# Attention and FFN in one kernel: a shorter lead-in, values sent in 128 rows, and another written order of the opening

## The chip, the cores and the metric

The kernel runs on one core of a Trainium2 chip. The core has a matrix engine (TensorE, PE in the profile; its weight loads are listed apart as PEld), a vector engine (VectorE, DVE), an activation engine (ScalarE, ACT), a general engine (GpSimd, POOL) and a queue processor that issues the DMA transfers here (SyncE, SP). Each engine works through its own list of instructions in order and waits on semaphores for the others. The metric is the device time of one execution in microseconds (us).

## The reference

The kernel computes attention for 8 batches, 8 heads, 576 positions and 64 channels per head, and then a two-layer FFN with GELU on the result. Heads 0 to 3 are local (each position sees the last 32), heads 4 to 7 are strided (each position sees every 32nd before it).

```python
scores = scale * np.matmul(q, k.transpose(0, 1, 3, 2))
mask_local = (rel >= 0) & (rel < stride)
mask_strided = (rel >= 0) & (pos[None, :] % stride == pos[:, None] % stride)
scores = np.where(masks[None, :, :, :], scores, -1000000000.0)
...
attn = np.exp(scores)
attn = attn / (np.sum(attn, axis=-1, keepdims=True) + 1e-09)
attn_out = np.matmul(attn, v).astype(np.float32)
...
x = np.ascontiguousarray(attn_out.transpose(0, 2, 1, 3)).reshape(B * S, H * D)
h = x @ w_in
g = 0.5 * h * (1.0 + erf(h * inv_sqrt2))
return (g @ w_out).astype(np.float32)
```

x has 4608 rows of 512 channels; w_in is 512 x 2048 and w_out 2048 x 512, all in float32.

## The kernel before

The 4608 rows are cut into 9 tiles of 512. For a tile the FFN goes through 16 slices of 128 hidden channels. For each slice `ffn_h` multiplies into the bank H (lines 655 to 657: 4 channel blocks times 3 products, since each float32 operand is split into a high and a low part so that the fast matmul keeps the precision), `ffn_g` applies GELU, and `ffn_o` multiplies into four banks O (lines 694 to 696, 12 matmuls). This is the bulk of TensorE's work. The 16 slices of the weights come by one DMA each (`load_w`, ws, 1 MB) and are split on chip by ScalarE and VectorE (`split_w`, lines 155 to 170, five steps: lead, word, other, high part, low part).

The attention of a tile must be done before its FFN. For every tile but the first, local heads are computed by `band_job` and strided heads on VectorE (`strided_qk`, line 526, and `strided_av`, line 571). The first tile has its own path, since TensorE has nothing else to do then. Its local heads run in four jobs (`local_job`): scores (L289) from qk, softmax on VectorE and ScalarE (L247 to L268), transposes (L295), copies (L297) and the product with the values (L303, `jv`, from vl). Its strided heads run on TensorE too: scores (L416) in two halves from qka, softmax (L425 to L439), transposes (L443), copies (L445), the product with the values va (L459, 64 small matmuls in the program), a transpose on VectorE (L464), and the split into the high part dh (L467, ScalarE) and the low part dl (L470, VectorE). After that the first H can start.

The values of the local heads are laid out by the host as `vl`: for each block of queries 96 keys (`LK`, 64 of the block and 32 before it) by 512 numbers, 192 KB. Blocks 0 to 3, those of the first tile, are loaded one by one (`load_jv`); later tiles load four at once (`load_values`, line 229).

Up to slice 16 the order of work on four of the engines is written by hand, in the table `START`. Each word is one step: w0 is the load of weight slice 0, q0 and v0 loads of local job 0, S and B the loads of the strided heads' q, k and v of the first tile, K1 and V1 those of the next tile's keys and values, E the strided heads' first q and k, L0 the next step of local job 0, a0 and b0 steps of the two halves, A0 of the strided product, c0 a step of the split of weight slice 0, f0 a step of the FFN with slice 0, s, x and y steps of the next tile's local heads, u and r steps of the strided ones. Each step issues its instructions on the engines that it needs, so the table sets the order within each engine's list, SP's queue of DMAs among them. GpSimd's order is not in it. Ahead of the table stand some matmuls on zeros, the lead-in (line 780), and the making of masks.

Eight semaphores tell of the landing of SP's DMAs in turn, so a DMA also waits for the one eight before it when that has not landed.

Of the kernel before, what the change touches and what calls it, by code (L numbers as in the profile page):

```python
# [24 lines left out]
P = 128  # L25
# [20 lines left out]

NB = 16
START = """
    q0 q2 L0 S0 q3 q1 L0 L2 w1 L2 L0 L2 v2 a0 L0 L0 v0 w0 L0 b0 L0 a0 L2 a0 B0 L2 L3 b0 w2 L1 L0 L2 a0 b0 L2
    L0 a0 L1 b0 v1 v3 L1 a0 b0 L2 a0 a0 L0 L1 L3 b0 b0 b0 a0 L1 b0 L0 L3 c0 c0 L3 a0 b0 b0 L3 a0 L1 A0 c0 A0  # L50
    w9 c1 A0 c1 A0 L1 L2 c0 c1 A0 L3 L1 L3 w3 c0 L2 E L2 c2 L1 L3 c1 c1 L1 L3 c2 K1 L3 L1 L3 c2 w5 f0 c3 f0
    f0 w4 f0 c2 c3 f1 c2 f1 c3 f1 c3 c4 s1 w7 f2 f1 c3 c4 c4 f2 f2 V1 f3 f3 c4 c5 w6 L4 f3 f0 c4 c5 f3 L5 w8
    c5 L5 c6 L4 e f1 f4 f2 f4 c5 c5 f4 f4 c6 c7 c6 w11 L6 f5 c7 c6 f5 c7 f2 f5 f3 c6 L4 w10 c7 f6 u0 c7 c8
    c8 f6 f5 f6 c8 c9 u0 c9 u0 w13 L5 L7 f7 f6 f4 u0 u0 c8 c8 L6 f5 f7 c9 c9 f8 u0 f7 u0 c10 f7 f8 f8 c10 c9
    f8 c10 c10 w12 u0 c11 c11 c10 L7 w14 u0 L6 c11 f6 f9 u0 f9 c11 f9 u1 L7 f7 c11 f10 f9 u1 w15 c12 c12 u1
    f10 f10 f8 f10 c13 u1 c13 c12 c12 f11 u1 u1 f9 c12 f11 f11 c13 c13 f11 c13 c14 u1 u1 x1 G0 c14 K2 f12
    f13 u1 c14 c14 f12 g0 f12 f12 c14 c15 f10 c15 c15 f13 c15 f13 r0 c15 f11 f13 f12 f14 f14 f14 r0 f14 f15
    y1 f15 r0 r0 u1 f15 y1 f15 r0 f13 f14 r0 f15 f15 r0 r0 r0 r0
""".split()

TOP_V = [6]
# [21 lines left out]
def attn_ffn_kernel(ctx: ExitStack, tc: tile.TileContext, qk, vl, qka, va, qs, ks, vs, w, out):  # L83
# [37 lines left out]
    def rows(j):  # L121
        return slice(j * D, (j + 1) * D)
# [5 lines left out]
    def slot(name, shape, dtype=F32):  # L128

        return wpool.tile(shape, dtype, name=name, tag="w")  # L130
# [72 lines left out]
    def load_jv(x):  # L203
        assert x < JPT
        if not vbig:
            vbig.append(slot("vl_0", [P, 4 * DM])[:LK, 0:JPT * 2 * HL * D].rearrange("p (j c) -> p j c", j=JPT))
        jv[x] = vbig[0][:, x].rearrange("p (a h d) -> p a h d", a=2, h=HL)
        nc.sync.dma_start(vbig[0][:, x], vl[x].rearrange("p a h d -> p (a h d)"))

# [14 lines left out]
    def load_values(t, after=None):  # L224

        js = range(t * JPT, (t + 1) * JPT)
        assert not jv
        b = both(f"vl_{t}")[:LK, 0:JPT * 2 * HL * D].rearrange("p (j c) -> p j c", j=JPT)
        pace(nc.sync.dma_start(b, vl[js[0]:js[0] + JPT].rearrange("j p a h d -> p j (a h d)")), after)
        for x in js:  # L230
            jv[x] = b[:, x % JPT].rearrange("p (a h d) -> p a h d", a=2, h=HL)
# [44 lines left out]
    def local_job(x, bank, dve=0, pn=-1):  # L276

        s = pt = bank[0].tile([P, DM], F32, name=f"S_L{x}", tag=bank[1])
        p, pts = buffers(f"L{x}", pn)
        nb = 2 * N2  # L280
        blocks = [slice(i * LK, (i + 1) * LK) for i in range(nb)]
        qv = jq[x][:, 0:nb * LU].rearrange("p (i t) -> p i t", t=LU)
        kv = jq.pop(x)[:, nb * LU:].rearrange("p (i t) -> p i t", t=LK)
        msk = [mask0 if LPLACE[2 * x + i % 2][1] == 0 else mask for i in range(nb)]
        steps = softmax_parts(blocks, P, lambda i: s[:, blocks[i]], lambda i: msk[i], p,
                              *small(f"L{x}"), dve)
        for i, cs in enumerate(blocks):
            for j in (i % 2, 1 - i % 2):
                nc.tensor.matmul(s[rows(j), cs], qv[rows(j), i, :], kv[rows(j), i, :], start=True, stop=True)  # L289
        for st in steps:  # L290
            yield
            st()
        yield
        for i, cs in enumerate(blocks):
            nc.tensor.transpose(pt[:LK, i * P:(i + 1) * P], p[:, cs], ident)  # L295
        yield
        nc.scalar.copy(pts[:LK, 0:nb * P], pt[:LK, 0:nb * P])  # L297
        yield
        xv = s[:, 0:N2 * P].rearrange("p (a q) -> p a q", a=N2)
        for i in range(nb):  # L300
            pr, a = divmod(i, 2)
            for j in range(2):
                nc.tensor.matmul(xv[rows(j), pr, a * LU:(a + 1) * LU], jv[x][:, a, 2 * pr + j, :],  # L303
                                 pts[:LK, i * P + j * LU:i * P + (j + 1) * LU], start=True, stop=True)
        jv.pop(x)
        yield
        t, c0 = divmod(x * P, TT)
        dst = [a[:, :, c0:c0 + P] for a in x_loc(t)]
        yield from to_x(*dst, xv)
# [6 lines left out]
    def band_job(x, bt, sx):  # L316

        QB = STRIDE  # L320
        i = x % JPT
        s = [t[:, i * P:(i + 1) * P] for t in sx[x // JPT]]
        qv = jq[x][:, 0:2 * N2 * LU].rearrange("p (r a t) -> p r a t", r=N2, a=2)
        kv = jq.pop(x)[:, 2 * N2 * LU:].rearrange("p (r a t) -> p r a t", r=N2, a=2)
        head = [(h % 2, slice(h // 2 * 2 * QB, (h // 2 + 1) * 2 * QB)) for h in range(HL)]
        for h in range(0, HL, 2):
            for g in range(P // QB):
                a, b = divmod(g, 2)
                for j in range(2):
                    nc.tensor.matmul(s[j][g * QB:(g + 1) * QB, head[h][1]],  # L330
                                     qv[rows(j), h // 2, a, b * QB:(b + 1) * QB],
                                     kv[rows(j), h // 2, a, b * QB:(b + 2) * QB],
                                     start=True, stop=True, tile_position=(j * D, g * QB))
# [24 lines left out]
        tv = pt.rearrange("p (c q) -> p c q", c=2)
        for g in range(P // QB):
            for c in range(2):  # L360
                kb = g % 2 + c
                nc.sync.dma_start(bt[kb * QB:(kb + 1) * QB, g, :], tv[g * QB:(g + 1) * QB, c, :])
        yield
        if i == 0:
            sx["x"] = score_banks(f"x{x // JPT}")
        xv = [t[:, i * P:(i + 1) * P] for t in sx["x"]]
        bv = bt.rearrange("p (a b) (h q) -> p a b h q", a=2, h=HL)
        for r in range(N2):
            for a in range(2):
                for j in range(2):  # L370
                    nc.tensor.matmul(xv[r][rows(j), a * LU:(a + 1) * LU], jv[x][:, a, 2 * r + j, :],  # L371
                                     bv[:LK, a, :, 2 * r + j, :], start=True, stop=True)
        jv.pop(x)

# [400 lines left out]
    zero = const.tile([P, 32], F32, name="zero")  # L775
    nc.vector.memset(zero, 0.0)
    lead_in = ps_h.tile([P, TT], F32, name="lead_in", tag="H")
    for i in range(75):
        h = i % HL
        nc.tensor.matmul(lead_in[h * 32:(h + 1) * 32, 0:8], zero[rows(0), :], zero[rows(0), 0:8],  # L780
                         start=True, stop=True, tile_position=(0, h * 32))
# [239 lines left out]
def lay_out(q, k, v, w_in, w_out):  # L1021
# [25 lines left out]
    def by_row(a):  # L1047
# [6 lines left out]
    wi = w_in.reshape(H, D, NF, P)  # L1054
    wl = wi[:HL].reshape(HL // 2, 2 * D, NF, P).transpose(2, 1, 0, 3)
    ws = wi[HL:].reshape(HL, D // 32, 32, NF, P).transpose(3, 0, 2, 1, 4).reshape(NF, HL * 32, D // 32, P)
    w = np.concatenate([wl, ws, w_out.reshape(NF, P, DM // P, P)], axis=2).reshape(NF, P, 2 * DM)
    return {
        "qk": np.concatenate([by_channel(pick(q, tq)), by_channel(pick(k, tk))], axis=2),
        "vl": pick(v, tk).transpose(0, 2, 1, 3, 4),  # L1060
        "qka": np.concatenate([qa, ka], axis=2), "va": va.reshape(NA, 4 * 32, -1),
        "qs": by_row(q), "ks": by_row(k), "vs": by_row(v),
        "w": np.ascontiguousarray(w).view(np.int64),
# [20 lines left out]
```

## Time and profile before

| | |
|---|---|
| median of three runs | 864.9 us (860.49, 866.51, 864.9) |
| profiled execution, its own time | 864.71 us |
| its span, first to last instruction | 862.9 us |
| mean granted clock of TensorE | 0.987 |
| bytes by DMA | 66.71 MB, 77 GB/s over the span |

The page draws the span in 40 slices of 21.6 us, one digit each, the busy share in tenths. The first two slices are the opening:

```profile
PE   6699999999999999999999999999999999999997
...
PEclk9699999999999999999999999999999999999999
DMA  9974322022301131211220222022101410101001
```

In a timeline, a group of instructions is one row: start, length, engine, line, operation, tiles, and in brackets how long its engine was idle ahead of it and which instruction ended that. "Issue" stands where nothing in the profile ended it. A matmul on plain float32 is two records for one row of the program (the 64 matmuls of L459 are 128), a transpose or a matmul on the split operands is one.

### The profile page before, as it was taken

The page shows a single profiled execution, that of the slowest core. Times are in us where ns is not written, and L with a number is a line of the kernel's source. Part 1 is how long each engine was busy: PE and PEld are TensorE (multiplying, and loading weights), DVE is VectorE, ACT ScalarE, POOL GpSimd, SP SyncE. Part 2 cuts the span into 40 slices and gives each one's busy share as a digit, 9 for nine tenths or more (in the row PEclk, how much of TensorE's full clock was granted, in tenths as well). Part 3 has the DMA queues.
Part 4 walks back from the last instruction along what each step waited for, and adds up shares of the span by engine and source line. Part 5 has one row for each costly group of instructions (what it writes and reads, how often), then busy time and mean ns, then how long its engine had stood idle before and what let it go on. Part 6 is the DMA issues. An engine that isn't in the chain of part 4 may idle for free.

```text
span 862.9 us, 17996 instructions
## 1 busy us (share of the span) xinstructions
PE 839.4 (97%) x5546; PEld 691.2 (80%) x5546; DVE 674.2 (78%) x4643; ACT 444.3 (51%) x864; POOL 18.1 (2%) x88
## 2 busy tenths in 40 slices
PE   6699999999999999999999999999999999999997
PEld 5587787887887888888888888888888888888886
DVE  4679977997799979996999899979998899621110
ACT  5689956653565336643665265545662466332222
POOL 5000000000000000000000000000000000000000
PEclk9699999999999999999999999999999999999999
DMA  9974322022301131211220222022101410101001
GB/s 300 323 257 163 147 98 86 7 68 75 108 7 60 26 110 54 68 37 63 85 62 14 90 86 67 14 91 87 56 14 36 139 44 14 35 7 43 1 0 50
DMA packets 33857, 66.71 MB, mean 77 GB/s; under 512 B 5984, under 2 KB 15840, under 8 KB 33632
## 3 DMA queue, kind: packets, MB, share of 16 engines
q1 hardware_dynamic: 33760, 65.56, 23.4%
q8 instruction: 44, 0.72, 0.3%
q14 instruction: 53, 0.43, 0.2%
HBM read 51.90 MB, written 9.44 MB: 71 GB/s over the span
## 4 chain that ended last, share of the span: by engine, by line
PE 81%; DVE 12%; DMA 4%; ACT 2%; issue 1%; SPq 0%; DVEq 0%; ACTq 0%
PE H L655 13%; PE H L656 13%; PE H L657 13%; PE O L696 13%; PE O L694 13%; PE O L695 13%; DVE junk L526 3%; DVE acc L571 3%; PE S_x L371 2%; DMA ws<-in_w_dram 2%; DVE gl L668 2%; PE S L330 1%; DMA qka<-in_qka_dram 1%; DMA sq<-in_qs_dram 1%; DVE w L170 1%
## 5 line engine op out<-in xcount | busy, mean ns | idle before, releaser
L571 DVE SCALAR_TENSOR_TENSOR acc<-sv,sc,acc 128x64 f32<-128x64 f32 x1104 | 229.5, 280 | 1.0
L696 PE MATMUL O<-w,gl 128*128 128x512 f32 x576 | 224.3, 389 | 0.0
L695 PE MATMUL O<-w,gh 128*128 128x512 f32 x576 | 224.2, 389 | 0.0
L694 PE MATMUL O<-w,gh 128*128 128x512 f32 x576 | 224.2, 389 | 0.0
L664 ACT ACTIVATE H<-H 128x512 f32<-128x512 f32 x144 | 83.9, 583 | 257.8 <-PE H L657 250.9
L668 DVE TENSOR_TENSOR gl<-H,gh 128x512 fp32r<-128x512 f32 x144 | 99.0, 687 | 120.7 <-ACT gh L666 119.8
L526 DVE CUSTOM_DVE_ANT_0 junk<-sq,sk 128x64 f32<-128x64 f32 x1232 | 192.7, 219 | 0.0
L666 ACT CAST gh<-H 128x512 fp32r<-128x512 f32 x144 | 84.6, 587 | 118.3 <-PE O L695 113.6
L696 PEld LDWEIGHTS O<-w,gl 128*128 128x128 f32 x576 | 108.2, 188 | 22.6
L694 PEld LDWEIGHTS O<-w,gh 128*128 128x128 f32 x576 | 108.1, 188 | 22.4
L695 PEld LDWEIGHTS O<-w,gh 128*128 128x128 f32 x576 | 108.1, 188 | 22.3
L655 PE MATMUL H<-dh,w 128*128 128x512 f32 x288 | 115.2, 400 | 3.6 <-DVE gl L668 2.3
L656 PE MATMUL H<-dl,w 128*128 128x512 f32 x288 | 112.9, 392 | 0.0
L657 PE MATMUL H<-dh,w 128*128 128x512 f32 x288 | 112.8, 392 | 0.1
L655 PE MATMUL H<-xh,w 128*128 128x512 f32 x288 | 112.2, 389 | 0.0
L656 PE MATMUL H<-xl,w 128*128 128x512 f32 x288 | 112.1, 389 | 0.0
L657 PE MATMUL H<-xh,w 128*128 128x512 f32 x288 | 112.1, 389 | 0.0
L526 DVE DVE_READ_ACCUMULATOR2_ANT sc<- 128x1 f32 x1232 | 102.5, 83 | 0.0
L655 PEld LDWEIGHTS H<-dh,w 128*128 128x128 f32 x288 | 54.3, 189 | 17.6 <-DVE gl L668 4.0
L664 ACT ACT_TABLE_LOAD x51 | 65.4, 1283 | 0.9
L657 PEld LDWEIGHTS H<-dh,w 128*128 128x128 f32 x288 | 54.3, 189 | 12.4 <-DVE w L170 0.8
L655 PEld LDWEIGHTS H<-xh,w 128*128 128x128 f32 x288 | 54.2, 188 | 11.5
(115 smaller groups left out, 756.5 us busy)
## 6 DMA issues: line engine op xcount, KB each, us to landing
ws<-in_w_dram SPq DMA_DIRECT2D x16, 1023.8 KB, 11.0
qk<-in_qk_dram SPq DMA_DIRECT2D x8, 1280.0 KB, 5.8
out_dram<-ob SPq DMA_DIRECT2D x32, 256.0 KB, 2.4
vl<-in_vl_dram SPq DMA_DIRECT2D x8, 768.0 KB, 5.7
sk<-in_ks_dram SPq DMA_DIRECT2D x8, 576.0 KB, 4.6
sv<-in_vs_dram SPq DMA_DIRECT2D x8, 576.0 KB, 3.7
band<-PT_L SPq DMA_DIRECT2D x224, 16.0 KB, 1.8
sq<-in_qs_dram SPq DMA_DIRECT2D x4, 448.0 KB, 3.6
```

The source lines that it names most:

```text
L371: nc.tensor.matmul(xv[r][rows(j), a * LU:(a + 1) * LU], jv[x][:, a, 2 * r + j, :], bv[:LK, a, :, 2 * r + j, :], start=True, stop=True)
L526: nc.vector.tensor_tensor_reduce(junk, sq[vi, "q"][:, r0 + r, :], sq[vi, "k"][:, c, :], 1.0, 0.0, ALU.mult, ALU.add, ss[u][:, r, c:c + 1])
L571: nc.vector.scalar_tensor_tensor(acc[:, r, :], sq[vi, "v"][:, c, :], wgt, acc[:, r, :], ALU.mult, ALU.add)
L655: nc.tensor.matmul(hp, w1[f][:, 0, c, :], xh, start=(i == 0), stop=False)
L656: nc.tensor.matmul(hp, w1[f][:, 0, c, :], xl, start=False, stop=False)
L657: nc.tensor.matmul(hp, w1[f][:, 1, c, :], xh, start=False, stop=(i == NC - 1))
L664: gelu[n] = nc.scalar.activation(hp, hp, AF.Gelu)
L666: nc.scalar.copy(gh, hp)
L668: nc.vector.tensor_tensor(gl, hp, gh.bitcast(F32), ALU.subtract)
L694: nc.tensor.matmul(o, gh[:, sl], w2[f][:, 0, :], start=(f == 0), stop=False)
L695: nc.tensor.matmul(o, gh[:, sl], w2[f][:, 1, :], start=False, stop=False)
L696: nc.tensor.matmul(o, gl[:, sl], w2[f][:, 0, :], start=False, stop=(f == NF - 1))
```

## The change

Four edits. The lead-in has 34 matmuls, not 75. The host lays out 128 rows per block of values: the 96 keys, then the first 32 of them again; so the loads fill all 128 partitions (256 KB each), and the matmuls read the first 96 as before. And the table `START` is another: the same steps in another order, with three more of the strided steps `r0`.

```diff
-    for i in range(75):
+    for i in range(34):
...
-            vbig.append(slot("vl_0", [P, 4 * DM])[:LK, 0:JPT * 2 * HL * D].rearrange("p (j c) -> p j c", j=JPT))
+            vbig.append(slot("vl_0", [P, 4 * DM])[:, 0:JPT * 2 * HL * D].rearrange("p (j c) -> p j c", j=JPT))
...
-        b = both(f"vl_{t}")[:LK, 0:JPT * 2 * HL * D].rearrange("p (j c) -> p j c", j=JPT)
+        b = both(f"vl_{t}")[:, 0:JPT * 2 * HL * D].rearrange("p (j c) -> p j c", j=JPT)
...
-                nc.tensor.matmul(xv[rows(j), pr, a * LU:(a + 1) * LU], jv[x][:, a, 2 * pr + j, :],
+                nc.tensor.matmul(xv[rows(j), pr, a * LU:(a + 1) * LU], jv[x][:LK, a, 2 * pr + j, :],
...
-                    nc.tensor.matmul(xv[r][rows(j), a * LU:(a + 1) * LU], jv[x][:, a, 2 * r + j, :],
+                    nc.tensor.matmul(xv[r][rows(j), a * LU:(a + 1) * LU], jv[x][:LK, a, 2 * r + j, :],
...
-    q0 q2 L0 S0 q3 q1 L0 L2 w1 L2 L0 L2 v2 a0 L0 L0 v0 w0 L0 b0 L0 a0 L2 a0 B0 L2 L3 b0 w2 L1 L0 L2 a0 b0 L2
+    q0 q2 S0 q3 L0 L0 q1 L2 L0 L2 a0 L0 v0 L0 L2 L0 b0 w0 v2 L2 L3 b0 a0 a0 b0 w2 L2 w1 L0 L0 L2 a0 a0 L1 a0
...
+    vt = pick(v, tk).transpose(0, 2, 1, 3, 4)
...
-        "vl": pick(v, tk).transpose(0, 2, 1, 3, 4),
+        "vl": np.concatenate([vt, vt[:, 0:P - LK]], axis=1),
```

Three places show what the table moves. The first is TensorE's list from its start. The tiles S_L0 to S_L3 are the scores of the four local jobs, A0 and A1 the two halves of the strided heads. Before:

```order
L780 MATMUL lead_in_135<-zero_133 32x8 x75
L289 MATMUL S_L0_319<-qk_0_91 64x96 x8
L289 MATMUL S_L2_341<-qk_0_91 64x96 x8
L416 MATMUL A0_0_371<-qka_0_331 32x32 x32
L416 MATMUL A1_0_410<-qka_0_331 32x32 x32
L295 MATMUL S_L0_319<-ident_85,pbig_87 96x128 x4
L289 MATMUL S_L3_454<-qk_0_91 64x96 x8
L289 MATMUL S_L1_473<-qk_0_91 64x96 x8
L295 MATMUL S_L2_341<-ident_85,P_L2_342 96x128 x4
L303 MATMUL S_L0_319<-pbig_87,vl_0_369 64x64 x8
L443 MATMUL A0_0_371<-ident_85,va_0_332 128x128 x2
L443 MATMUL A1_0_410<-ident_85,va_0_332 128x128 x2
```

After, the same stretch of TensorE's list:

```order
L780 MATMUL lead_in_135<-zero_133 32x8 x34
L289 MATMUL S_L0_283<-qk_0_91 64x96 x8
L289 MATMUL S_L2_300<-qk_0_91 64x96 x8
L416 MATMUL A0_0_322<-qka_0_278 32x32 x32
L416 MATMUL A1_0_364<-qka_0_278 32x32 x32
L289 MATMUL S_L3_401<-qk_0_91 64x96 x8
L295 MATMUL S_L0_283<-ident_85,pbig_87 96x128 x4
L289 MATMUL S_L1_439<-qk_0_91 64x96 x8
L303 MATMUL S_L0_283<-pbig_87,vl_0_356 64x64 x8
L295 MATMUL S_L2_300<-ident_85,P_L2_301 96x128 x4
L443 MATMUL A0_0_322<-ident_85,va_0_279 128x128 x2
L443 MATMUL A1_0_364<-ident_85,va_0_279 128x128 x2
```

The lead-in is shorter by 41 rows; the scores of job 3 stand ahead of the first transposes now, and the first product with the values (L303) ahead of the second transposes. In both lists the 64 matmuls of L459 follow, then two groups of L295 and three of L303, then the first H.

The second place is SP's queue of DMAs, from the second pair of qk on (qk are the local heads' q and k, ws weight slices, vl and va values of the local and the strided heads, sq and sk the strided heads' rows for VectorE; the first number behind ws is the slice). Before:

```order
L201 DMA qk_0_91<-in_qk_dram 128x640 x2
L135 DMA ws_1_355<-in_w_dram 128x4095
L208 DMA vl_0_369<-in_vl_dram 96x512 x2
L135 DMA ws_0_407<-in_w_dram 128x4095
L400 DMA va_0_332<-in_va_dram 128x1024
L135 DMA ws_2_471<-in_w_dram 128x4095
L208 DMA vl_0_369<-in_vl_dram 96x512 x2
L135 DMA ws_9_619<-in_w_dram 128x4095
L135 DMA ws_3_662<-in_w_dram 128x4095
L500 DMA sq_1_666<-in_qs_dram 128x256 x4
L500 DMA sk_1_671<-in_ks_dram 128x256 x4
L220 DMA qk_1_701<-in_qk_dram 128x4x640
```

After:

```order
L201 DMA qk_0_91<-in_qk_dram 128x640 x2
L208 DMA vl_0_356<-in_vl_dram 128x512
L135 DMA ws_0_397<-in_w_dram 128x4095
L208 DMA vl_0_356<-in_vl_dram 128x512
L135 DMA ws_2_423<-in_w_dram 128x4095
L135 DMA ws_1_426<-in_w_dram 128x4095
L208 DMA vl_0_356<-in_vl_dram 128x512
L400 DMA va_0_279<-in_va_dram 128x1024
L135 DMA ws_9_597<-in_w_dram 128x4095
L208 DMA vl_0_356<-in_vl_dram 128x512
L220 DMA qk_1_616<-in_qk_dram 128x4x640
L135 DMA ws_3_623<-in_w_dram 128x4095
```

The first values and weight slice 0 come first; va stands behind three weight slices and three values rather than two and two; and the next tile's keys (L220) stand ahead of weight slice 3 and of sq and sk.

The third place is VectorE's list from L464 to the last step of weight slice 0. Before:

```order
L464 STREAM_TRANSPOSE qka_0_331<-A3_0_553 128x256
L166 CAST w_0_646<-ws_0_407 128x1024
L162 SCALAR_TENSOR_TENSOR ws_1_355<-ws_1_355 128x1024
L470 TENSOR_TENSOR dl_0_624<-qka_0_331,dh_0_623 128x4x64 x4
L170 TENSOR_TENSOR w_0_646<-ws_0_407,w_0_646 128x1024
```

After:

```order
L464 STREAM_TRANSPOSE qka_0_278<-A3_0_510 128x256
L162 SCALAR_TENSOR_TENSOR ws_1_426<-ws_1_426 128x1024
L166 CAST w_0_595<-ws_0_397 128x1024
L470 TENSOR_TENSOR dl_0_581<-qka_0_278,dh_0_580 128x4x64 x4
L170 TENSOR_TENSOR w_0_595<-ws_0_397,w_0_595 128x1024
```

Two steps of the weights' split have changed places; the strided heads' low part and the last step of slice 0 stand where they did.

More of the change, by code (lines that the diff above doesn't have):

```diff
@@ L48 @@
 START = """
-    q0 q2 L0 S0 q3 q1 L0 L2 w1 L2 L0 L2 v2 a0 L0 L0 v0 w0 L0 b0 L0 a0 L2 a0 B0 L2 L3 b0 w2 L1 L0 L2 a0 b0 L2
[L50 to L58, printed above, removed]
+    q0 q2 S0 q3 L0 L0 q1 L2 L0 L2 a0 L0 v0 L0 L2 L0 b0 w0 v2 L2 L3 b0 a0 a0 b0 w2 L2 w1 L0 L0 L2 a0 a0 L1 a0
+    L1 L1 b0 v3 a0 b0 b0 a0 L0 b0 L3 b0 B0 L1 a0 b0 L0 L2 L2 L0 L1 L3 a0 c0 c0 L3 b0 b0 L3 a0 A0 A0 L1 c0 c1
+    c1 A0 L2 c1 c0 w9 v1 A0 L1 A0 L3 K1 c0 L3 w3 L2 L1 L1 L3 c2 E c2 L2 c1 c1 L1 L3 L3 L1 c3 L3 c2 f0 w4 f0
+    w5 f0 c3 c2 f0 f1 c2 f1 f2 c3 f1 w7 c3 f1 c4 s1 f2 c3 c4 c4 c5 f3 f2 V1 f3 L5 L4 c4 c5 c4 f2 w6 c5 c6 f0
+    f3 e f1 L4 L5 c5 f4 w8 w13 f4 f4 c5 f3 w10 c6 L4 f4 c7 c6 f5 c6 f2 c6 c7 c7 c7 f5 f3 f6 u0 c8 f5 c7 L6
+    c8 f6 w11 f5 f6 u0 c9 u0 u0 L7 c9 L5 f7 c8 w12 f6 f4 u0 c8 L6 f5 c8 f7 f8 f7 c9 u0 c9 u0 f7 c10 c9 c10
+    f8 f8 c10 c11 c10 c11 f8 w14 L6 L7 u0 c10 f6 c11 f9 f9 c11 f9 u1 L7 f7 c11 c12 c12 f9 w15 u1 u0 u1 u0
+    f10 f10 f10 f10 f8 c12 u1 u1 c13 c13 c12 f11 c13 c12 u1 f9 f11 f11 c14 x1 c13 c13 c14 f11 G0 K2 f12 f12
+    f12 u1 f12 u1 c14 c15 f10 u1 r0 f13 g0 c14 c14 c15 c15 f13 c15 f13 c15 f11 f13 f12 f14 f14 f14 r0 r0 r0
+    f14 f15 y1 u1 r0 f15 r0 y1 f15 f15 f13 r0 r0 f14 r0 r0 r0 r0 f15 f15 r0
 """.split()
```

## The prediction

> **What bounds the kernel now.** I read the page's head first, then one answer that cuts the span into stages (from, to and length in us; busy us of each engine with its instructions in brackets; then PE's granted clock, the share of the DMA engines, GB/s).
>
> ```profile
> span 862.9 us, 17996 instructions
> ...
> PE 839.4 (97%) x5546; PEld 691.2 (80%) x5546; DVE 674.2 (78%) x4643; ACT 444.3 (51%) x864; POOL 18.1 (2%) x88
> ```
>
> ```profile
> 0.00:36.00 36.00, 20.70 (x555) 17.08 (x555) 18.78 (x77) 21.30 (x61) 11.86 (x54) 0.75 0.89 290
> 36.00:60.00 24.00, 23.88 (x219) 19.00 (x220) 17.89 (x36) 19.36 (x37) 0.00 (x0) 0.95 0.97 357
> 60.00:100.00 40.00, 37.63 (x165) 30.58 (x164) 37.88 (x174) 37.88 (x60) 0.25 (x2) 1.00 0.33 118
> 100.00:200.00 100.00, 99.13 (x609) 80.97 (x608) 89.80 (x613) 59.57 (x106) 2.50 (x6) 1.00 0.23 77
> 200.00:862.00 662.00, 658.02 (x4004) 543.58 (x4002) 509.84 (x3746) 306.19 (x603) 3.53 (x26) 1.00 0.17 53
> ```
>
> From 36 us on, TensorE (PE) is hardly ever idle: 0.12 us up to 60, 2.37 up to 100, 0.87 up to 200, 3.98 after that, together 7.3. The idle time lies in the opening: 36.0 - 20.7 = 15.3 us before the first FFN matmul. So the question is when the dense stream of FFN matmuls begins; whatever starts it earlier moves the end by as much, as long as VectorE (DVE) keeps up. The list of waits of PE in the first 60 us says what held it:
>
> ```profile
> PE A L459 <- issue: 5.5, 1, 5.5
> PE A L416 <- DMA qka<-in_qka_dram: 3.3, 1, 3.3
> PE S_L L303 <- DMA vl<-in_vl_dram: 1.9, 1, 1.9
> ```
>
> The longest wait is for nothing that the profile shows ("issue"). The timeline of PE in the opening places it (start, length, in brackets the idle time before):
>
> ```profile
> 3.69 2.83 PE L289 MATMUL S_L<-qk 64*64 64x96 f32 x32 [0.49 <-DMA qk<-in_qk_dram]
> 9.83 1.94 PE L416 MATMUL A<-qka 64*32 64x32 f32 x128 [3.32 <-DMA qka<-in_qka_dram]
> 11.69 1.09 PE L295 MATMUL S_L<-ident,pbig 128*96 128x128 f32 x4
> 12.71 2.44 PE L289 MATMUL S_L<-qk 64*64 64x96 f32 x32
> 15.07 0.65 PE L295 MATMUL S_L<-ident,P_L 128*96 128x128 f32 x4
> 17.65 0.85 PE L303 MATMUL S_L<-pbig,vl 96*64 96x64 f32 x16 [1.93 <-DMA vl<-in_vl_dram]
> 19.15 1.09 PE L443 MATMUL A<-ident,va 128*128 128x128 f32 x4 [0.65 <-DVE rs_L L259]
> 21.33 1.78 PE L459 MATMUL A<-va 32*32 32x64 f32 x107 [1.09 <-DVE va L445]
> 28.58 0.49 PE L459 MATMUL A<-va 32*32 32x64 f32 x21 [5.46 <-issue]
> ```
>
> L459 stops in the middle of 128 identical matmuls, with no semaphore between them. The queues of DMA tell why, for 16.3 to 26.1 us and then for 26.1 to 27.2:
>
> ```profile
> q1 hardware_dynamic: 678, 3.16, 101.7%
> q14 instruction: 1, 0.01, 0.2%
> ```
>
> ```profile
> q1 hardware_dynamic: 62, 0.45, 101.5%
> q8 instruction: 1, 0.02, 5.8%
> ```
>
> ```profile
> q8 instruction: 44, 0.72, 0.3%
> ```
>
> Instructions come by DMA too. PE's 5546 matmuls and 5546 weight loads in the 44 packets of q8 (last fence, the whole span) are 252 instructions to a packet of 16 KB, about 126 matmuls with their loads. While the data queue kept the engines full (101.7%), no q8 packet ran for ten microseconds; one ran after 26.1, and PE went on at 28.58. I read the pause as PE out of code: the rows above add up to 150 (lead-in) + 32 + 128 + 4 + 32 + 4 + 16 + 4 + 107 = 477 matmuls before it.
>
> [...]
>
> **The change part by part.** Fewer lead-in matmuls: 41 fewer at L780, two records each (75 give 150), so 82 records, about 1.2 us of the 2.2 they took. On the path this is nothing: PE then waits for q and k until 3.69 anyway. But every later matmul moves 82 places towards the front of the code, and the places where PE runs out stay. Both orders have the same work ahead of the first H, so matmul 477 of the new code is 559 of the old. L459 ends at 477 + 21 = 498; two L295 and three L303 groups add 4 + 16 + 4 + 16 + 16 = 56, to 554; so the end of that block now falls at the fifth matmul of the first H. The block before, 128 earlier (349 + 82 = 431 in old places; old L459 is 371 to 498), ends in the middle of L459.
>
> What the pause costs on the path is seen behind it: L464 waits for L459, and from there runs a chain on DVE to the first H.
>
> ```profile
> 29.13 1.44 DVE L464 STREAM_TRANSPOSE qka<-A 128x256 f32<-128x256 f32 x4 [5.37 <-PE A L459]
> ...
> 35.92 0.80 PE L655 MATMUL H<-dh,w 128*128 128x512 f32 x1
> ...
> 36.31 1.15 ACT L157 CAST lead<-ws 128x1024 f16<-128x1024 bf16 x1
> ...
> 36.52 0.63 PE L656 MATMUL H<-dl,w 128*128 128x512 f32 x1
> ...
> 36.94 0.63 PE L657 MATMUL H<-dh,w 128*128 128x512 f32 x1
> ...
> 40.21 0.39 PE L656 MATMUL H<-dl,w 128*128 128x512 f32 x1
> ...
> 40.44 0.39 PE L657 MATMUL H<-dh,w 128*128 128x512 f32 x1
> ```
>
> The chain keeps its instructions and nearly its order (L162 of the second weight now comes before L166 of the first instead of behind it, the same sum), so it keeps its 35.92 - 29.07 = 6.85 us. Without the pause the term is **-5.46 us**.
>
> Is the pause gone or only elsewhere? Two blocks matter. In the old run the block that PE missed was entered between L295 at 15.07 and L303 at 17.65, and its successor's packet ran at 26.1 to 27.2: 8.5 to 11 us later. In the new order the boundary inside L459 belongs to a block entered at the end of L416, about 11.7 us; PE needs the next one at about 23, 11.3 us later. The one at the first H was entered inside L459 at about 23 and is needed some 9 us later. So both are met or missed by little: between 0 and 2.5 us, and I take **+0.5** for the two, near the lower end, since the packet comes after the data that was queued when it was asked for, and there is less time lost on that data, as follows.
>
> Values with 128 rows (the matmuls still read 96, so PE's work is unchanged): four first loads of 192 KB become 256 KB, 0.26 MB more, and each later one 1 MB instead of 768 KB. What 96 rows do is read from the rates while they are in flight:
>
> ```profile
> 9.00:11.00 2.00, 1.17 (x88) 1.17 (x92) 0.59 (x2) 1.05 (x6) 1.89 (x5) 1.00 1.03 425
> 12.00:16.00 4.00, 3.72 (x40) 2.98 (x38) 2.46 (x16) 2.46 (x9) 2.13 (x12) 1.00 1.03 245
> 17.00:20.00 3.00, 1.70 (x20) 1.46 (x20) 2.67 (x17) 2.27 (x11) 0.00 (x0) 0.67 1.02 418
> 21.00:25.00 4.00, 1.78 (x107) 1.51 (x108) 1.97 (x3) 3.73 (x4) 0.00 (x0) 0.50 1.06 251
> ```
>
> The engines are full in all four stretches, yet the last column falls from 420 to 250 GB/s in two of them. These are where, by the bytes issued ahead, the 96-row loads move: 3.4 MB stand ahead of the first pair on the old queue and 6.4 MB ahead of the second, which the rates put at 12 and 21 us. With 128 rows, the shape of all other loads, I expect 418 throughout. The 8 us at 250 would then take 4.8, less 0.6 for the added bytes: 2.6 us of queue time. On the path it is cover, not gain: PE's wait for vl (1.9) lies ahead of L443, which waits for DVE as well.
>
> The order on the DMA queue decides when va is there, which L459 needs:
>
> ```profile
> 6.91 0.62 SPq L400 DMA_DIRECT2D va<-in_va_dram  x1
> ```
>
> ```profile
> va<-in_va_dram SPq DMA_DIRECT2D x1, 512.0 KB, 13.8
> ```
>
> That is 20.7 in the old run; L459 then waited for DVE until 21.33. The new queue has ahead of and with va: 4 x 320 KB of q and k, qka 1024, three values of 256, three weights of 1024, va 512, together 6.8 MB; the old one 5.4. The first 10 us moved 2.63 MB:
>
> ```profile
> 0.00:5.00 5.00, 3.52 (x166) 3.43 (x168) 0.57 (x4) 1.49 (x2) 3.63 (x22) 1.00 0.56 185
> 5.00:10.00 5.00, 1.68 (x32) 1.39 (x32) 2.42 (x19) 2.92 (x16) 4.17 (x17) 1.00 0.94 341
> ```
>
> The other 4.2 MB take 10.0 us at 418 GB/s, so the last byte is at 20.0. Landing comes later by some 2 us (qka's 1.7 MB were through at 7.3 by these rates, and L416 started at 9.83), so 22.0: **+0.7** against 21.33. At 250 GB/s it would be 16.8 us, landing at 28.8, 7.5 later than 21.33. I take the first, because queue and shape are those of the 418 stretch. The other loads that moved: w3 now stands behind the second tile's keys (1.28 MB, 3.1 us), with 10.5 MB ahead and with it, so it lands near 31, when its first use (L157 at 36.31 before, 5 us earlier now) begins; no cost, though with little to spare. Those keys wait on SP's queue until PE has read the first tile's (the L289 that ended at 15.15); w3 and the strided heads' q and k queue behind them, while the 8.1 MB issued ahead last to 23 us. Three more steps of the strided heads (0.8 each by the planner's units) enter the opening on DVE, bounded by 0 and 2.4 us; DVE is idle 10.2 us between 100 and 200, so 0.
>
> The clock of PE. The first H ran at 0.42 us per matmul (36.52 to 36.94), later ones at 0.23; the granted clock's mean of 0.95 from 36 to 60 means 2.4 us at half, to about 38.4. Between no slow matmul and 6.8 us of them, H loses 1.3 us less to 2 us more than now; I take **+0.7**, since the step came early in the profiled run. The shorter lead-in adds nothing: with 75 matmuls the clock was low already, four L295 taking 1.09 us at 11.69, as long as four L443 at 19.15, where the clock column falls to 0.5, and 0.65 only at 15.07 (the 1.00 that the column shows at 9 to 11 us does not fit those 1.09).
>
> [...]
>
> Sum: 864.7 (the profiled execution; its span is 862.9) - 5.46 + 0.5 + 0.7 + 0.7 = 861.1. The three runs before have a median of 864.9, 0.2 above, so I say **861 us**.
>
> **The rivals.**
> - The pause stays, at another place: the block inside L459 or at the first H comes as late as it did. For it: the queue is as full as before. Against: both are asked for 9 to 11 us ahead. 861.1 - 0.5 + 5.5 = 866. The same time comes out if the pause belongs to L459 itself and not to code; against that stands the long absence of a q8 packet.
> - [...] I give it 0.05 of the 0.18 below.
> - More is gained: the clock opens at once (2.0 better than my term), no block is late (0.5), va lands as DVE ends (0.7), and a third of the 2.37 us between 60 and 100 goes with weights that come earlier (0.8): 861.1 - 4.0 = 857. With all of the 2.37 it is 855.5.
> - Slower: 128 rows do not cure the queue (250 GB/s remains) and va lands at 28.8, so L459 starts 7.5 us later instead of 0.7: 861.1 + 6.8 = 868. It decides against the change once va lands after 21.3 + 5.5 - 1.2 = 25.6 us. For it: the cause of the 250 is read from timing alone; against: 128-row loads ran at 425 just before.
>
> **How the numbers follow.** My forecast (858.5 to 864) 0.54, the pause stays 0.18, more is gained 0.18, slower 0.1. The range 856 to 867 leaves out the far ends of the last two, under 2 in 10. One per cent of 864.9 is 8.6 us, about what a measurement of this kernel can tell from no change; below 856.3 lies 0.1, the outer half of "more is gained"; above 873.5 lies 0.03, if pause and late va meet; 0.87 is within.
>
> **What would show it.** Right: no idle "issue" of several us before an A matmul of L459; the first H near 31 instead of 35.92; DMA near 400 GB/s all through 9 to 30 us; idle time from 100 us on as before. Wrong: a wait of L459 on va beyond 22 us, a pause of PE inside the first H or L459 with a q8 packet just before its end, or a first H that is early while idle time between 60 and 200 us grows by what was gained.

## The result and the profile after

| | before | after |
|---|---|---|
| median, eight runs of each | 864.51 us (860.49 to 866.51) | 858.74 us (856.2 to 861.81) |
| profiled execution, its own time | 864.71 us | 859.48 us |
| its span | 862.9 us | 857.7 us |

The ratio of the times is 0.9939, with a 95% interval of 0.9917 to 0.9961: the changed kernel is 0.4 to 0.8% faster, 5.8 us between the medians. That is inside the 1% that the prediction called no change, and 2 us below its forecast of 861.

First the head of the changed kernel's page, then the answer by stages (columns as before: from, to, length; busy us of PE, PEld, DVE, ACT, POOL with their instructions; granted clock, DMA share, GB/s).

```profile
span 857.7 us, 17839 instructions
...
PE 839.0 (98%) x5464; PEld 690.4 (80%) x5464; DVE 675.1 (79%) x4643; ACT 443.9 (52%) x864; POOL 18.2 (2%) x88
```

```profile
0.00:36.00 36.00, 24.61 (x486) 19.70 (x487) 23.15 (x82) 24.25 (x65) 11.98 (x54) 0.72 0.94 355
36.00:60.00 24.00, 21.86 (x216) 17.34 (x215) 17.60 (x38) 20.40 (x37) 0.00 (x0) 1.00 0.83 323
60.00:100.00 40.00, 39.82 (x229) 32.37 (x227) 38.23 (x179) 36.40 (x58) 0.25 (x2) 1.00 0.34 116
100.00:200.00 100.00, 99.95 (x564) 81.77 (x560) 91.36 (x636) 58.20 (x107) 2.59 (x7) 1.00 0.22 72
200.00:857.00 657.00, 652.75 (x3980) 539.21 (x3978) 504.77 (x3714) 304.61 (x599) 3.40 (x25) 1.00 0.17 56
```

TensorE does the same work (839.0 us against 839.4); all that moved is its idle time. In the opening it fell from 15.3 to 11.4 us. From 36 to 60 us it rose from 0.12 to 2.14, from 60 to 100 it fell from 2.37 to 0.18, from 100 to 200 from 0.87 to 0.05, and after that it is 4.25 against 3.98. The timeline of PE in the opening:

```profile
0.98 1.13 PE L780 MATMUL lead_in<-zero 64*32 64x8 f32 x68 [0.98 <-DVE zero L776]
9.72 1.31 PE L416 MATMUL A<-qka 64*32 64x32 f32 x123 [3.10 <-DMA qka<-in_qka_dram]
11.33 0.32 PE L416 MATMUL A<-qka 64*32 64x32 f32 x5 [0.30 <-issue]
20.62 0.87 PE L443 MATMUL A<-ident,va 128*128 128x128 f32 x4 [2.94 <-DVE va L439]
22.41 1.96 PE L459 MATMUL A<-va 32*32 32x64 f32 x128 [0.91 <-DVE va L445]
31.08 0.80 PE L655 MATMUL H<-dh,w 128*128 128x512 f32 x1
34.23 0.58 PE L656 MATMUL H<-xl,w 128*128 128x512 f32 x1
34.65 0.39 PE L657 MATMUL H<-xh,w 128*128 128x512 f32 x1
```

L459 runs through its 128 records; the pause of 5.46 us is gone. The first H starts at 31.08 instead of 35.92, and runs at about half speed (a matmul every 0.43 us, later every 0.23) for 8 matmuls instead of 6. A small pause is left at L416, behind 68 + 32 + 123 = 223 records. That is 254 ahead of the 477 of the old trace. In all the runs the stops lie behind 223, 349 or 350, and 476 or 477 records, 126 to 128 from one to the next; a block is counted as 128 records from here on, and this stop is two blocks ahead of 477 within two records.

Of the wait list from 36 to 60 us one row matters; from 60 to 200 us no wait was left to list.

```profile
PE H L655 <- DVE gl L668: 2.1, 1, 2.1
```

The rates of the DMA queue, in four stretches of 5 us:

```profile
10.00:15.00 5.00, 4.70 (x151) 3.93 (x139) 2.61 (x7) 0.91 (x4) 4.18 (x17) 0.57 1.02 420
15.00:20.00 5.00, 2.69 (x28) 1.90 (x25) 2.87 (x23) 4.22 (x19) 0.00 (x0) 0.74 1.01 411
20.00:25.00 5.00, 3.46 (x145) 2.81 (x147) 4.33 (x15) 4.91 (x10) 0.00 (x0) 0.60 1.02 401
25.00:30.00 5.00, 3.53 (x32) 2.35 (x32) 5.00 (x10) 5.00 (x13) 0.00 (x0) 0.50 1.04 395
```

There are no stretches of 250 GB/s any more. The values va were issued at 10.48 and took 11.6:

```profile
va<-in_va_dram SPq DMA_DIRECT2D x1, 512.0 KB, 11.6
```

### The profile page after: what moved, and what is told of

Its sections match the earlier page's. It is cut to its first block, busy times and chain, and to the rows that moved or that the text cites. A ratio compares the mean times of both kernels' runs of the same rounds, so it can differ in the third digit from the quotient of the medians.

```text
span 857.7 us, 17839 instructions
## 1 busy us (share of the span) xinstructions
PE 839.0 (98%) x5464; PEld 690.4 (80%) x5464; DVE 675.1 (79%) x4643; ACT 443.9 (52%) x864; POOL 18.2 (2%) x88
## 3 DMA queue, kind: packets, MB, share of 16 engines
q1 hardware_dynamic: 34912, 67.92, 23.1%
## 4 chain that ended last, share of the span: by engine, by line
PE 79%; DVE 13%; ACT 3%; DMA 2%; issue 1%; SPq 0%; DVEq 0%; ACTq 0%
PE H L655 13%; PE H L656 13%; PE H L657 13%; PE O L695 12%; PE O L694 12%; PE O L696 12%; DVE junk L526 4%; DVE acc L571 3%; PE S_x L371 2%; DVE gl L668 2%; PE S L330 1%; DMA ws<-in_w_dram 1%; DMA qka<-in_qka_dram 1%; DVE ws L162 1%; ACT lead L157 0%
## 5 line engine op out<-in xcount | busy, mean ns | idle before, releaser
L695 PEld LDWEIGHTS O<-w,gh 128*128 128x128 f32 x576 | 108.2, 188 | 22.3
```

The costliest lines, as they stand in the source:

```text
L695: nc.tensor.matmul(o, gh[:, sl], w2[f][:, 1, :], start=False, stop=False)
```

## The experiments

Three edits (lead-in, rows of the values, written order) make eight kernels. With the two ends, all eight were run; three more lead-ins and second runs of three kernels came besides. One table holds the results; the pause (the longest "issue" of PE ahead of the first H; shorter ones are told below) and the first H are those of the one profiled execution. Ratios are against the kernel before, on the same chip; the medians come from several chips, so kernels are better compared by the ratios.

| kernel | lead-in / rows / order | median us | ratio, 95% interval | pause, where | first H |
|---|---|---|---|---|---|
| before | 75 / 96 / old | 864.51 | 1 | 5.46, L459 | 35.92 |
| e2_before_lead34 | 34 / 96 / old | 863.39 | 0.9991, 0.9975 to 1.0007 | none | 30.69 |
| e6_before_lead60 | 60 / 96 / old | 861.4 (one run) | | 4.72, L303 | 31.98 |
| e3_before_rows128 | 75 / 128 / old | 862.07 | 0.9970, 0.9957 to 0.9982 | none | 30.33 |
| e12_rows128_again | the same | 861.57 | 0.9976, 0.9965 to 0.9987 | 2.72, L459 | 32.11 |
| e5_before_order_34_128 | 34 / 128 / old | 859.69 | 0.9944, 0.9929 to 0.9960 | none | 30.22 |
| e11_34_and_128_again | the same | 859.79 | 0.9955, 0.9940 to 0.9971 | none | 29.60 |
| e7_after_order_75_96 | 75 / 96 / new | 866.27 | 1.0019, 1.0006 to 1.0032 | 4.60, L459 | 39.37 |
| e4_after_rows96 | 34 / 96 / new | 859.62 | 0.9946, 0.9931 to 0.9960 | none | 33.17 |
| e1_after_lead75 | 75 / 128 / new | 861.85 | 0.9965, 0.9953 to 0.9977 | 4.27, L459 | 35.92 |
| after | 34 / 128 / new | 858.74 | 0.9939, 0.9917 to 0.9961 | 0.30, L416 | 31.08 |
| e10_after_again | the same | 858.85 | 0.9943, 0.9924 to 0.9961 | none | 31.06 |
| e8_after_lead0 | 0 / 128 / new | 859.39 | 0.9943, 0.9928 to 0.9958 | 4.33, L303 | 33.54 |
| e9_after_lead50 | 50 / 128 / new | 857.32 | 0.9929, 0.9912 to 0.9945 | none | 32.04 |

### Does the number of lead-ins set the place of the pause?

The changed kernel with the old lead-in, and the kernel before with the new one, each with this line alone:

```diff
-    for i in range(34):
+    for i in range(75):
```

> The kernel after with 75 lead-in matmuls instead of 34, nothing else. If TensorE runs out of code at a fixed number of matmuls (477 of the trace's records), the pause comes back, again behind the 107th of the 128 matmuls of L459, and lasts until the next code packet has landed: the block before it is entered with the first L303 at about 15.5 us, the data queued by then needs until 23 to 26 us, so a pause of 3 to 5 us and a time of 862 us (860.5 to 863.5). If the pause belonged to the old order or to the 96-row values, the lead-in is worth nothing: 858.7 us, no pause.

> The kernel before with 34 lead-in matmuls, nothing else. If the pause hangs on the place in the code: none behind the 107th matmul of L459, perhaps one of up to 2.5 us in the middle of it (record 349 is there now), the first H near 31.5 us instead of 35.9, 860 us (859 to 862). If the pause hangs on the order or the values: 864.5 us, the pause where it was.

The pause came back in e1, at the same record of L459 as in the kernel before, although the order and the rows were the new ones:

```profile
22.57 1.77 PE L459 MATMUL A<-va 32*32 32x64 f32 x107 [0.91 <-DVE va L445]
28.61 0.49 PE L459 MATMUL A<-va 32*32 32x64 f32 x21 [4.27 <-issue]
```

It has a second, shorter stop, behind 150 + 32 + 128 + 16 + 4 + 16 + 4 = 350 records, 127 ahead of the other, so one block within a record:

```profile
16.35 0.57 PE L303 MATMUL S_L<-pbig,vl 96*64 96x64 f32 x12 [0.60 <-issue]
```

The first H was back at 35.92, and the ratio was 0.9965 against 0.9939 (861.85 us against 858.74; the intervals just overlap): as expected. In e2 the pause was gone and the first H came at 30.69, 5.2 us earlier, but the time hardly changed (863.39, interval of the ratio up to 1.0007). The expectation was right about the pause and wrong about the time. The stretch 36 to 60 us of e2, the two longest waits of PE in it, and ACT's row behind them show where it went:

```profile
36.00:60.00 24.00, 21.15 (x213) 16.69 (x212) 16.44 (x33) 19.05 (x36) 0.00 (x0) 1.00 0.97 344
```

```profile
PE H L655 <- DVE w L166: 1.9, 1, 1.9
PE H L657 <- DVE w L170: 0.5, 1, 0.5
```

```profile
43.82 1.11 ACT L157 CAST lead<-ws 128x1024 f16<-128x1024 bf16 x1 [4.19 <-DMA ws<-in_w_dram]
```

PE is idle 2.85 us there, 0.12 before: the FFN overtook its weights. A slice of weights for which ACT waited 0.27 us in the kernel before (L157 at 44.37) holds it for 4.19 us here, with ACT's GELU steps queued behind it. With 96 rows the queue did not bring the weights as early as PE could now use them; with 128 rows and all else as in e2 (e5, below), PE is idle 0.12 us there. This is the account of one execution, of 862.22 us, 2.5 less than the profiled one before. The twelve of e2 reach from 860.3 to 866.52, four of them above 866, and none of those four was profiled; so why the median gained only about 1 us is explained in part.

Two more lead-ins, 60 with the rest of the kernel before and 0 with the rest of the changed one, the same line edited:

> The kernel before with 60 lead-in matmuls: 30 records fewer ahead of everything. If TensorE runs out of code at record 477, L459 runs through without a pause (L464 starts near 23.5 us instead of 29.1) and the pause stands behind the fifth or so of the 16 matmuls of the first L303 group after L459, for 5 us or more, since its block is now entered only at the start of L459; 864 us (862 to 866). If the pause belongs to L459: it stays behind the 107th of its matmuls.

> The kernel after with no lead-in matmuls at all: 68 records fewer. If code position decides, fewer is not better: record 349 stands now right behind L459 and its block is asked for only at the start of L459 (22.4 us), so a pause of some 5 us or more at the first L303 behind L459, first H near 35 us, 862 us (860.5 to 864). If the lead-in only has a cost or a warming of its own: no pause, 858.7 us, or a little later by a colder clock.

Both pauses came where the count of records puts them. In e6, then in e8:

```profile
22.84 0.48 PE L303 MATMUL S_L<-PT_L,vl 96*64 96x64 f32 x4
28.04 0.91 PE L303 MATMUL S_L<-PT_L,vl 96*64 96x64 f32 x12 [4.72 <-issue]
```

```profile
24.01 0.37 PE L303 MATMUL S_L<-PT_L,vl 96*64 96x64 f32 x1
28.71 1.12 PE L303 MATMUL S_L<-PT_L,vl 96*64 96x64 f32 x15 [4.33 <-issue]
33.54 0.50 PE L655 MATMUL H<-dh,w 128*128 128x512 f32 x1
34.34 0.40 PE L655 MATMUL H<-dh,w 128*128 128x512 f32 x1
```

In e6 the list reads 120 + 32 + 128 + 4 + 32 + 4 + 16 + 4 + 128 + 4 + 4 = 476 records before the stop, one less than 477; in e8 32 + 128 + 16 + 4 + 16 + 16 + 4 + 4 + 128 + 1 = 349, which is 477 - 128. So a pause of the same kind also falls in the matmuls with L303, and has nothing to do with L459 itself. Both kernels were faster than expected, though (861.4, one run, against 862 to 866, and 859.39 against 860.5 to 864). A pause of 4 to 5 us behind L459 lies beside work of VectorE and ScalarE that the first H waits for anyway: from the end of L459 to the first H the changed kernel takes 31.08 - 24.37 = 6.7 us, e8 with its pause of 4.33 takes 33.54 - 24.08 = 9.5, so some 2.8 us of the pause showed. And the first H of e8 runs at full speed almost from its start (0.40 us, against 0.63 in the changed kernel).

### Which of the pauses is met in time?

> The changed kernel with 50 lead-in matmuls. Theory (TensorE runs out after a fixed number of matmul records, each block being asked for two blocks ahead): 32 records more than with 34, so the boundaries fall at record 445, in the L303 groups ahead of the first H (100 + 32 + 128 + 32 + 4 + 32 + 16 + 4 + 4 = 352 up to L459 would put L459 at 353 to 480, so 349 falls in L443 and 477 behind the 125th of L459). Expected: pause of about 4 us behind the 125th matmul of L459 and first H between 33 and 35.5. Time 860 to 862, since the pauses of other lead-ins cost 0.7 (none at all) to 3 us (75) against the 34. Rival (the lead-in matters only by its length): no pause, 859.

The expectation counted 352 records ahead of L459; the list has 320, so record 477 is the fifth of the second L303 group after it (448 + 16 + 4 + 4 + 5). There was no pause there, or anywhere:

```profile
23.37 1.97 PE L459 MATMUL A<-va 32*32 32x64 f32 x128 [0.91 <-DVE va L445]
29.90 1.12 PE L303 MATMUL S_L<-pbig,vl 96*64 96x64 f32 x16 [0.29 <-ACT pbig L297]
```

A miss in place and time (857.32 against 860 to 862). It also limits the theory: the place where PE can run out is fixed, but whether it does depends on when the packet comes. The packets of q8 answer that. Cut in windows of 0.1 us, the traces give the windows in which they start; each then takes about 1 us (5.8% of 16 engines over 1.1 us in the prediction's second fence of queues). The last column is where PE stood.

| kernel | record | packet starts at | PE at the end of its code |
|---|---|---|---|
| before | 477 | 26.1 | stops at 23.1, goes on at 28.58 |
| e1_after_lead75 | 350 | 13.8 | stops at 15.8, goes on at 16.35 |
| | 477 | 26.0 | stops at 24.3, goes on at 28.61 |
| e6_before_lead60 | 476 | 25.3 | stops at 23.3, goes on at 28.04 |
| e7_after_order_75_96 | 350 | 14.7 | stops at 16.2, goes on at 17.44 |
| | 477 | 29.6 | stops at 27.5, goes on at 32.07 |
| e8_after_lead0 | 349 | 26.0 | stops at 24.4, goes on at 28.71 |
| e12_rows128_again | 350 | 13.1 | stops at 14.9, goes on at 15.71 |
| | 477 | 22.3 | stops at 22.1, goes on at 24.78 |
| e3_before_rows128 | 477 | 19.5 | passes at 23.0 |
| after | 223 | 8.9 | stops at 11.0, goes on at 11.33 |
| | 349, 477 | 15.3, 26.8 | passes at 23.3, at 33.0 |
| e9_after_lead50 | 349, 477 | 14.8, 27.3 | passes at 23.8, at 30.2 |

In all ten stops PE goes on 2.4 to 2.7 us after the start of the packet; where the packet started 2.9 us or more ahead, there is no stop. In the kernel before, the wait of 1.93 us ahead of the first L303, which the view puts down to vl, stands behind record 350 as well, and ends at 17.65, 2.7 us after a packet of 14.9; it may have been code too. When a packet is asked for, no view shows. That it happens as PE leaves the block two before fits the first packet of q8: it starts at 7.3 in the kernel before, with 75 lead-ins, where record 93 (349 less two blocks) lies in the lead-in, at 8.9 in the changed kernel, with 34, where it lies in the first L289, and at 12.9 in e8, with none, where it lies in L416.

The changed kernel has its code for L459 at 15.3, and none is fetched for the next 11 us, as in the old one; but none is needed. Its q8 shows nothing in the answer by queue for 16 to 25 us either:

```profile
q1 hardware_dynamic: 1008, 3.62, 101.4%
q14 instruction: 1, 0.01, 0.2%
```

Fetching ran ahead of use here: in the changed kernel the packet of 15.3 was needed at 23.3, and of all its code only the 0.30 us at L416 showed as a wait. Records 223, 350 and 477 each saw a stop that ended behind a single packet of 16 KB (0.72 MB in 44 packets), and in e1, e6, e7 and e8 4.3 to 4.7 us of waiting showed.

### What do the rows do?

The kernel before with 128 rows, and the changed kernel with 96; the edit in one of them, the other its reverse (line 229, the matmuls, and the host's layout):

```diff
-        b = both(f"vl_{t}")[:LK, 0:JPT * 2 * HL * D].rearrange("p (j c) -> p j c", j=JPT)
+        b = both(f"vl_{t}")[:, 0:JPT * 2 * HL * D].rearrange("p (j c) -> p j c", j=JPT)
...
-        "vl": pick(v, tk).transpose(0, 2, 1, 3, 4),
+        "vl": np.concatenate([vt, vt[:, 0:P - LK]], axis=1),
```

> The kernel before with values of 128 rows, nothing else. If 96 rows slow the whole queue, the rate stays near 410 GB/s from 9 to 29 us and the code packet behind the same data runs some 2.5 us earlier (near 23.5 us instead of 26.2), the pause stays behind the 107th matmul but shrinks to about 3 us: 862 us (861 to 863.5). If the rows don't matter but the bytes do, the packet runs 0.6 us later: 865 us.

> The kernel after with values of 96 rows, nothing else. If 96 rows slow the queue (250 GB/s while they move), va and the weights land 2 to 3 us later, L459 starts near 24.5 us instead of 22.4 and the code for the middle of L459 comes late too: 861 us (859.5 to 863). If they don't matter: 858.5 us, first H at 31.

The rates rose as expected. In e3 they were:

```profile
10.00:15.00 5.00, 5.00 (x155) 4.56 (x144) 1.93 (x7) 2.01 (x7) 4.07 (x17) 1.00 1.03 417
15.00:20.00 5.00, 2.25 (x30) 1.65 (x26) 4.48 (x29) 4.40 (x20) 0.00 (x0) 0.84 1.03 415
20.00:25.00 5.00, 4.09 (x150) 3.15 (x148) 4.30 (x10) 4.91 (x7) 0.00 (x0) 0.50 1.01 408
```

The time of e3 was as expected (862.07 against 862), and its pause was not: expected 3 us, shown 0. The same kernel profiled again (e12, below) shows 2.72, so a single profile must not be read as the pause of every execution. In e4 the values came late, and L459 waited 2.50 us for them at 24.50, as expected, but no code was late; the first H came 2.1 us later than in the changed kernel, and the median, 859.62, was within the range expected. The ratio of 0.9946 against 0.9939, with intervals that overlap almost wholly, shows no loss by 96 rows there. In the other three pairs 128 rows have the lower ratio: 0.9970 against 1, 0.9944 against 0.9991 and 0.9965 against 1.0019.

```profile
24.50 1.96 PE L459 MATMUL A<-va 32*32 32x64 f32 x128 [2.50 <-DMA va<-in_va_dram]
```

### What does the order do?

All but the order in e5, the order alone in e7: in e5 the table `START` is the old one, in e7 the lead-in is 75 and the rows are 96.

> The kernel before with 34 lead-in matmuls and 128-row values: all of the change but the written order. Either edit alone took the pause away, so the two should not add up: no pause in L459, first H near 30.5 us, 862 us (860.5 to 863), and the rest to 858.7 is the order's. If the order is worth nothing: 858.7 us.

> The written order after, with 75 lead-in matmuls and 96-row values: the order alone. If code position and queue decide: the pause is back behind the 107th matmul of L459, which itself starts near 24.5 us for want of va, first H near 36 us, but no wait for weights behind it: 863.5 us (862 to 865). If the order alone is the gain: 858.7 us.

Lead-in and rows together, in the old order, gave 859.69, below the expected range and nearly all of the gain. The order alone made the kernel slower (866.27, the interval of the ratio wholly above 1), more so than the 862 to 865 expected. Its trace holds both mishaps at once, the values late and then the pause:

```profile
25.71 1.76 PE L459 MATMUL A<-va 32*32 32x64 f32 x107 [3.37 <-DMA va<-in_va_dram]
32.07 0.49 PE L459 MATMUL A<-va 32*32 32x64 f32 x21 [4.60 <-issue]
```

Yet the new order does something of its own. In every run with the old table but e2 PE was idle 2.4 us from 60 to 100, in e2 1.4; with the new one 0.2 to 0.5, and 1.4 in e7. In e5, for 36 to 60 and 60 to 100:

```profile
36.00:60.00 24.00, 23.88 (x225) 19.09 (x224) 17.66 (x43) 20.55 (x38) 0.00 (x0) 1.00 0.72 279
60.00:100.00 40.00, 37.63 (x219) 30.58 (x218) 39.20 (x181) 37.92 (x60) 0.25 (x2) 1.00 0.38 130
```

Lead-in and rows were expected to overlap, since each takes away the same pause. They did the reverse: from e3 to e5 the shorter lead-in brought 2.4 us although neither profile shows a pause. So three kernels were run again beside each other.

> The changed kernel again, beside the two that follow on the same chip, to size the written order by itself. Expected 859, with the first H near 31 and no pause in L459.

> The kernel before with 34 lead-in matmuls and 128 rows, in the old written order, again. Theory (the order has no worth of its own once lead-in and rows have changed): within 0.5 us of the changed kernel run beside it. Rival (the order is worth the 1 us of the first measurements): 0.8 to 1.2 us above it.

> The kernel before with 128 rows alone, 75 lead-in matmuls, again. Theory (nothing in the trace but the lead-in itself differs between this and the one with 34 and 128 rows, so the 2.4 us between their medians came from the spread of single runs): within 1 us of that kernel. Rival (the shorter lead-in is worth 2 us even where there is no pause): 2 to 3 us above it.

The changed kernel came out as expected (858.85, first H at 31.06). The 1.8 us between e12 and e11 stayed, nearer to the rival's 2 to 3 than to the theory's 1, and the rival's condition, no pause, did not hold. The trace of e12 has the cause, the pause that e3's one profile had happened to miss:

```profile
20.28 1.78 PE L459 MATMUL A<-va 32*32 32x64 f32 x107 [0.91 <-DVE va L445]
24.78 0.49 PE L459 MATMUL A<-va 32*32 32x64 f32 x21 [2.72 <-issue]
```

Between e11 and e10 lie 0.94 us, the rival's figure, but the two intervals of the ratio overlap (0.9940 to 0.9971 and 0.9924 to 0.9961). The order's worth in this company is about 1 us, and not established.

The profiles of e11 and e12 also show one reason why a pause can cost less than its length. The first H of e11 starts 2.51 us ahead of that of e12:

```profile
29.60 0.80 PE L655 MATMUL H<-dh,w 128*128 128x512 f32 x1
...
33.60 0.63 PE L655 MATMUL H<-xh,w 128*128 128x512 f32 x1
34.03 0.46 PE L656 MATMUL H<-xl,w 128*128 128x512 f32 x1
```

```profile
32.11 0.80 PE L655 MATMUL H<-dh,w 128*128 128x512 f32 x1
...
33.98 0.57 PE L656 MATMUL H<-dl,w 128*128 128x512 f32 x1
34.39 0.39 PE L657 MATMUL H<-dh,w 128*128 128x512 f32 x1
```

Both reach full speed at 34 us. The matmuls gained ahead of that moment run at about half speed (one every 0.43 us, behind it every 0.23), so 2.51 us of earlier start are worth about half, 1.26; the two profiled executions differ by 859.33 to 860.67, 1.34. Not every pair of executions shares that moment (last section).

## Why the prediction was right, point by point

- **The pause (-5.46).** Right: it was PE out of code, its place follows the count of records in five further runs (e1, e6, e7, e8, e12), and in the changed kernel it is gone. The rival that it belongs to L459 itself, the 0.05 of the prediction's 0.18, falls with e6 and e8. The 128 records that the prediction put between two blocks, against about 126 by its count of packets, agree with the stops, 126 to 128 from one to the next.
- **The two blocks at new places (+0.5).** The reason was too dark. It took the 8.5 to 11 us between the entry of a block and the packet in the old trace as the rule, and so saw both new blocks met or missed by little; its ground, that the packet comes behind all the data queued when it was asked for, does not hold. The packet at 15.3 ran about 4 us after the end of record 221 (11.33), while va, issued at 10.48, was queued until 22.1, and PE needed its code at 23.3, 8 us later; the one at 26.8 had 6 us to spare. The one loss was the 0.30 us at L416, at a third block that was not counted.
- **The values va (+0.7).** Estimated to land at 22.0; 10.48 + 11.6 is 22.1. L459 began at 22.41, though, 1.1 later than before, released by L445 on DVE and not by va: L443 already stood at 20.62 against 19.15, waiting for L439. So the term was 0.4 short, and DVE's new order set it: in e1 and e10, in the new order too, L443 starts at 20.98 and 20.41, in e3 and e5, with the same rows in the old order, at 19.26 and 19.16.
- **The clock (+0.7).** Eight slow matmuls instead of six are two times 0.2 (0.43 us each against 0.23), +0.4. No run shows the 6.8 us of slow matmuls at the upper end of its range: the longest stretch listed is 6.1 (e1, 35.92 to 42.05), that of the changed kernel 3.6 (31.08 to 34.65).
- **The first H.** Near 31 was said, 31.08 came.
- **No change later (0).** This is the step that failed. The idle time of 60 to 200 us was to stay, since DVE has 10 us to spare there; it fell from 3.24 to 0.23, and between 36 and 60 us a wait for gl of 2.0 us came up in its place. With +0.3 after 200 us the net is -0.7. The sign "idle time from 100 us on as before" did not come either (0.87 before, 0.05 after). It comes with the new order: in all seven profiles of the old order PE is idle 0.82 to 0.87 us from 100 to 200, in all seven of the new one 0.05 or less, with a pause and without. What came up instead differs between executions: a second profile of the changed kernel, e10, has 0.82 us idle from 36 to 60 where the first has 2.14:

```profile
36.00:60.00 24.00, 23.18 (x222) 18.45 (x221) 18.47 (x38) 20.70 (x37) 0.00 (x0) 1.00 0.86 334
```

Which of the moved steps does it was not taken apart. The three added r0 steps are not the reason for what went from 60 to 100 us. The two waits that made up the 2.37 us there are

```profile
70.97 0.47 PE L655 MATMUL H<-dh,w 128*128 128x512 f32 x1 [1.35 <-ACT gh L666]
96.72 0.50 PE L655 MATMUL H<-dh,w 128*128 128x512 f32 x1 [1.02 <-DVE gl L668]
```

and the first r0 comes later than both: in the old table it stands behind the first step of f13, whose H starts at 107.25 in the kernel before, in the new one behind the steps of f12, whose H starts at 100.09 in the changed kernel.

The span's sum is then 35.92 to 31.08 (-4.84), clock +0.4, 36 to 60 us +2.0, 60 to 200 -3.0, after that +0.3: -5.1, and the span fell by 862.9 - 857.7 = 5.2. The forecast was -3.6. Of the 1.6 between them 0.7 is the later idle time, 0.6 the opening (-4.84 for -5.46 + 0.5 + 0.7 = -4.26) and 0.3 the clock. Two parts of the rival "more is gained" came true: no block was late, and the idle time of 60 to 100 us went, all but 0.18 of it rather than a third, though not by earlier weights: e5 has them earlier (its fifth L157 runs at 40.95, not 44.37) and keeps its 2.37. Its other two parts, the clock and va, did not. The measured 858.74 is 0.24 above the lower end of the band of 858.5 to 864 and nearer to this rival's 857 than to 861. That it stayed in the band owes something to luck: in the profiled execution the new wait of 2.0 us from 36 to 60 made up for most of the 3.0 us of idle time that went after it, and neither was in the sum. The rival "slower" has its mechanism shown in e7, where rows and lead-in are left as before: va late and a pause, 866.27.

What stays open: why the packet that would be asked for at the end of record 349, near 15.5 us, waits 4 us in e3, about 7.5 in e12 and 10 in the kernel before and in e1. The full data queue is common to all of them (101.7% of the 16 engines from 16.3 to 26.1 us in the kernel before, 102.0% from 14 to 22 in e12, 98.5% to 109.8% in each us from 15 to 26 in e1, a DMA share of 1.03 from 15 to 20 in e3), and to the changed kernel (1.02 from 10 to 15), where the packet of 15.3 waited 4.

## What to carry to other kernels

An idle "issue" in the middle of identical instructions deserves a count of the instructions ahead of it: if the count stays put when the lead is changed, and a packet of the instruction queue stands just ahead of its end (2.4 to 2.7 us here), the engine is out of code. Some instructions fewer ahead then move the stop, to a place where the code is there in time (34 and 50 lead-ins here) or to another where it is not (60 in the old kernel, none in the new). A stall taken out of an opening is worth what the next limits leave of it, here the clock, the weights and VectorE: a first H 5.2 us earlier brought a ratio of 0.9991 where the weights were late, and 5.7 us earlier, with the rows mended, 0.9944. Edits that meet on one queue are to be tried together as well as one by one, since one of these was a loss alone, one next to nothing, and neither figure told their sum.

## What the runs showed of the hardware that was not expected

- The clock opened at the same 34 us in e11 and e12, whose first H lay 2.5 us apart, and in the changed kernel, between them, at 34.5; but other executions of two of these kernels, e3 and e10, opened at 35.2 and 35.1. In e1, with its first H at 35.92 as in the kernel before, 14 matmuls were slow where that kernel had 6. So the opening stood from 2 (e12, 34 behind 32.11) to 6 us (e1, 42.05 behind 35.92) after the first H, at no fixed distance from it; what sets its moment no run here shows.
- The loads of 96 rows cost the queue as a whole up to 40% of its rate in the stretches where they move, by an estimate from the bytes issued ahead: 245 and 251 GB/s in the kernel before, where 128 rows, with a third more bytes, kept 408 to 417 in e3.
- A packet of code took about 1 us to run but had been due, by the two-block reckoning, an estimate, for some 4 us (e8) to 13 us (e7) where PE stopped for more than 2 us, and PE went on only 2.4 to 2.7 us after its start, in all ten stops.
